# A new written order and a new list of VectorE-masked tiles in an attention and FFN kernel on one core

## The chip, the core and the metric

The kernel runs on one core of one Trainium2 chip. A core has five engines with a queue each, which work in the order of their queues: TensorE (PE; its weight loads are shown as PEld), VectorE (DVE), ScalarE (ACT), GpSimd (POOL) and SyncE (SP), which here only issues DMAs. The metric is the time of one execution on the device in microseconds (us); lower is better. Several runs are given by their median.

## The reference, cut to what matters

```
scores = (q @ k.T) / sqrt(64)                    # 8 batches, 8 heads, 576 rows, head size 64
thresh = max(scores, axis=-1) - tau              # tau = 0.02
scores = where(scores >= thresh, scores, -1e9)
attn   = softmax(scores)                         # over the keys
x      = (attn @ v), heads side by side          # 4608 tokens x 512
h      = max(max(x @ w1, x @ w2), x @ w3)        # 512 -> 768
out    = h @ w_out                               # 768 -> 512, float32
```

Only scores within 0.02 of their row's maximum survive.

## The kernel before, in words

**Tiling.** The structure repeats by batch: a batch has two quads of four heads. A quad's queries are cut into 9 chunks (the last batch is cut in two parts, line 34), and a chunk has two score tiles (r = 0 and 1, one for each pair of heads) of 128 rows by 576 keys. That makes 16 quads, 144 chunks and 288 score tiles. When both quads of a batch are done, its FFN follows: 18 hidden pieces (6 column blocks times w1, w2, w3) and three output pieces.

**The way of a score tile.** TensorE multiplies into one of four PSUM banks (`scores`, line 279). VectorE takes the row maximum (`maximum`, line 311). Then there are two ways. A *masked* tile (line 314: its digit in MASKED is 1) is copied to SBUF as z by VectorE while it takes the maximum; ScalarE takes the exponential of z (line 327); and VectorE multiplies z by (z >= exp(-tau)) and sums the row (`numerators`, lines 333 to 335). In the other way ScalarE reads the bank itself, with a Prelu that flattens all above the threshold (line 329), and takes the exponential and the sum in a second pass (line 337). So a masked tile has two passes on VectorE and one on ScalarE, the other kind one and two. After both tiles of a chunk VectorE takes the reciprocals, POOL multiplies z by them into P (bf16, line 346; six P buffers, four sets of z buffers), and SP turns the chunk's P by a DMA transpose into `ptq` (line 356). A product (`product`, line 358) needs all nine transposed chunks of its quad; VectorE and ScalarE evacuate it to x.

**What sets the order.** ORDER (line 38) is the program written out by hand, letter by letter; `issue` (line 596) emits one piece for each letter, and every engine gets its instructions in that order (`_Ordered`, line 80). On an engine's queue nothing overtakes. The letters by queue:

- TensorE: S score tile, T transposes of q or k (needed before the quad's first score tiles), O product, F first half and B second half of an FFN piece. The digit after S, T, O and F is the PSUM bank. A bank can be written again when its last reader is done.
- VectorE: m maximum, k mask and sum (masked tiles), r reciprocals, c evacuation of k, v maximum of hidden pieces, w evacuation of a product.
- ScalarE: e exponential or Prelu, n exponential and sum (other tiles), a evacuation of q, h evacuation of the first hidden piece, u of output pieces, x of products.
- POOL: p half of a P, q copies of q with its halves exchanged, y casts of v, z casts of the weights.
- SP: t transpose of a P, l one of eight loads of the next quads, g load of weights, o stores.

The letter n or k after an e must fit the tile's digit in MASKED, so the two lists belong together. An FFN piece of a batch can start only when the batch's four products are evacuated; the first needs 36 score tiles.

Of the kernel before, what the change touches and what calls it, by code (L numbers as in the profile page):

```python
# [21 lines left out]
FLAT = 2.0 ** -100  # L22

MASKED = """
101001010100010100100100100001010100000101000011000101010100000100100100
000000111101010100001000101000001100100011011000110011000010100010010001
000100110011000100111000010000101001001100011110000100100010010000111010
100100101111001001000001000110110001100001010111001110011100100001101100
"""


# [4 lines left out]
PBUFS = 6  # L36

ORDER = """
lllS0lmyS1eyS2lmlS3kelmnS0lmegS1repmgS2kyemnS3pT0meS1tmeymaS3S2knS0llremplekT3pnlrS1meqmnpmteprceT2qketS3pS0
anT1rmS2lpnmS3qlempntrcS2pekT1eptS0mnqmelprkalS3petS1mnS2qrmnS0lperlmpetkpeT3mnlS1pmetS2mpnremptekyS0nS2qmlT  # L40
1nzrcaemT1pS3ekpteS0mnS2yrmqelcplnS3rplnmS1tpemS2epmS0tepmS1nrS3mptekpT0erlekO2qtamnpS0melpmleS1kteT3rmnpS0l
nqmleprwnS1qeS2pmtnS0mpeO1czntrmnpS3wekT0permT2aptkeS0pxS3rcnS1gpmtnS2rpmepmetS0mqnO3qmegprnS2wynS0mS1etprmO
3epkeztxS2mewmpF3egS0kpeS2rnBmzF1tmhnkyS3egS2rpmBeF0pnvpBtemF1nkT3zBevF2akS0pghBmnF3tS1rvepBmnpS2F0rveqtS1mp
BmS3ezremF2pghkS1zetBmnF0vS3epgBnmF2pS1vetBmT0hS3rcpeF1S2rmpBmpteF0vpeBknS3ztF1nmS2vyeT3gzBmlO0hrlpalnpF1wle
T3ytBcnS0kS2nlmzO3nlrmeqlvelS2pS0rwxrmyF1npmS3gqBekqeF2vntpBmnS0pS1hmpgeS2mpeS3rmpeF0tmpeBrnS1pvS2tepmF0nzS3
metBrmpT2nS1vpaS3tnS0zmS2ermtpF1nkpnmS3eByrtmepkepF2lemlukS0utkBermnpoT1rekpoS0ecO3lupmtnpO1weoqurktpnS3T0xr
wS2mapoF1meT3qlS0cetBqmF3phS2kleqBmlF1nyF0lrnvBelpBrvS3yhpS2mnF1ptmS0epBmeF2ptvnF3BkeS1tvBnS0mhF2rmepS3rBepm
S1nytvF0peS3mpBnlmS2yetvT3eF1maS0lkBeqlS3mhlF2rmeplT1nlcpS0eBlrmpF1tnS3kpeBmnlO0qvernvtpT2S3wapS1nrmF2ptnS0m
qBempF3hS1kqteO2meykT0rxrBwpceS2yvnS0ylmF1nlS3pmelF2pmtBeBkpeS0vhlS3nrtmF1pS2mepBrlmeF3ptS0vepS2mnBtmF1evnT2
lS0kuS3lakS1onF2rmpemlepS0rkepBtmnpmF3erqktepT1uBuconqroS0yuS2pumoS1pT3mteS0ympeO2koayntmO3ewqelrkS1qxlT2wS0  # L50
rnmlpF3mlepcS1BleyF0tmphS2kpeBlmF3nF1lyveBtrknBpS0vhS2lpnrmF3S1pmetBpmeS0veS1tF2mnS3meBlmnF1F0lveBrelkpS2lBh
mF3npF1vBetkS0nrrBvpF2mhpS3BeptmS1nyvT0T3nrmO2parcyetpS0ewqS3mnO1pmeptkeS2qT3xwS0mayF1meqF3kBeqBrnvT2pS0hclS
1ynmtF3nS2mpBelmpF1elS0vetBmnF3rS2veplBmnpF1S0rhkptBemF3nprS2vleBpmS0tnpvF1emS3tuS2rkepS1nrF0mopnmepS3tmeS2p
rmBeptmeykS1yelS2mupS3lumO1temekT0oeF2ronwplakT3nT1qcS0nBpmnqtraS3peO1mqukuqonT0wS3rocpxS2lmeF0ptrF1mepBkpS3
thBremS0plvF2eptS3mS1ymeBlmF0pelS3veBmF2thS1keBknF0lmF3nlBveBlrknF2plS1rhvBnpmF3nS0pvtBepmF2rS1vtepBmpF0hT3k
tBerS2pavS1npF3mS0qmteBrmepO2vnpeS1twnS3mS0nF2meS1meBrmF0phS3knpBemO2eqvterkpT1xT0wS3caF2pnmT1qBtnrcF0pnvS3q
lBempF1lhS2rkyleBtmF0pvS3epBlrnmS1ypnvF2pterS3mpuS0meS2ptF1meymetS3knS0keBomnrmS2eplS3umpF0luroemptS2ekpT1em
T3oBakteqcT1nS2klaS3rmulpO1umoqeorkyeS0S2npmO3nprtwepmS1xpT0wtnmF2qS3ecpBlermF0qlhkS1pteBmnF2S3pvleBymlnF1vS
0eBtnmF2hS3keBlrmpF1nlvF0pnBlrpS2etvBynmS3S1hlrpmF2erpS0mteBpmeS3pvtnF0S1myeyF2pmeBktBeF3khT1vBaS2vnT0qS1rmp
O3meqcepS2wnF0tS1rnmpT3nmBpS2arvpS1temF3qeO0mpeketT2kxBnwS1clF0hrlmS2pnlBrkyeF3lmF1BrveqlBkpnF0lS2vhlBprmT3t  # L60
S1pvaS2pmeF0tS3mpeBkpteF1vnS2pmulS0moS1eF3metrmepS2knpS1S0nmBertmpekpS1nF2mertmpeS0kepS1mBuuqmtnS0keO3omeoku
O1urkoperowT2xpwT0cS3aqtS1nmF2qrF0myepBekS3yBhmF1pnS2vqteBmpnT0F3rcpelS2vBpnlS0mtphS1meS3mteF2knBmleS0lrnvpS
1ermF2plnS3pmteBpmF1eS0rveptBmnpF2kS3htBemF1nS0rvpleBmpF2nlrS3vpelT0mBtpaS1khS3qtmS0eqO2nmekerS3mpS1nmpO0ewt
ermpF2xwT3kpeF0cnBF1ntvT3BnkBarvS2phT3rrF0mqS1pceBmqtT3nS2pvS1ampS0eF3mpteF2mqeBkByeT1vhS0cT3pS2amF1qtnmF3qe
BkqBevS0nrF2vpT1rmupS3noS2cpnS0mpF1etmyeyrmpS2etkBepmnS3ktuS0urmF2peompnorS1kpeS3tmeS0BpmemteS1kuS0urS3kopnO
2ormepeO1pmnpweO0twrxmO2pxkS1eptS0xmnF3mS2teBkF0hmF1nBkS3ervF2peBmpBveS0ytF3hmS1F2emBkF0eBrvnpBrF1vphS3kpBtF
2mF0pveBytS3nyvO1kO2xrmF1xpBrkepS2BhmF3nptF0vepBF1ntvBS2hBmF3vS0eBrmpF1F2vpeBnS3thS0mBmF1eS3veBmnF0vO2urkepo
O1S0xpS3mF1tmekS0eBmweF3rkpnkuS2pnBorrmupteF0pF1hF2nopvF0tuvpF1rhF2pvF0tvF1phF2vF0tvF1hF2uvF0ovF3hoF1vF2vF0h
F3vF1vO2uoO0wF3xF1F2hF0vF1vF2hF0vF1vF2hF0vF1vF2hF0vF1vF2hF0vF1vF2hF0vBvF1uuooBF2uuouoo
"""  # L70


# [627 lines left out]
```

## Time and profile before

| | before |
|---|---|
| median of 3 runs | 466.03 us (464.69 to 467.4) |
| profiled execution, span from first to last instruction | 465.6 us |
| TensorE busy | 437.9 us (94%) |
| VectorE busy | 403.9 us (87%) |
| ScalarE busy | 394.0 us (85%) |
| GpSimd busy | 318.7 us (68%) |
| DMA packets | 87.44 MB, mean 188 GB/s |
| chain that ended last | PE 70%, DVE 11%, ACT 11%, issue 5%, DMA 2% |

The profile is of one execution. Its slices are 40 equal parts of the span, 11.64 us each; a digit is the busy share in tenths, and PEclk is the granted TensorE clock, in tenths of full speed. A group's row gives line, engine, operation, the tile written and those read, the count, then after the bar the busy time, the mean duration in ns, and the idle time just before, with what ended it. All instructions stand at L89, the line of the helper that records them, so they are told apart by tiles: `sc` scores, `z` and `unused` the outputs of the passes over a score tile, `ptq` the transposed P, `ph` and `po` the FFN's banks, `o` the product. Time of a queue's issuing is shown as SPq. The median is of other runs than the profiled one.

### The profile page before, as it was taken

How to read it: one execution, taken by the hardware profiler on the slowest of the kernel's cores; microseconds unless marked ns; L12 is line 12 of the kernel's file. 1: busy time of each engine (PE TensorE's matmuls, PEld its weight loads, DVE VectorE, ACT ScalarE, POOL GpSimd, SP SyncE). 2: the span in 40 equal slices, each digit the busy share in tenths (PEclk: the TensorE clock that was granted, in tenths of full speed). 3: DMA queues.
4: the chain of work that ended last, by engine and by line, in shares of the span. 5: the costliest groups of instructions: out<-in, count | busy, mean ns of one | idle time of the engine just before them, and what ended most of it. 6: DMA issues, size and time to landing. Idle time of an engine off the chain costs nothing.

```text
span 465.6 us, 14101 instructions
## 1 busy us (share of the span) xinstructions
PE 437.9 (94%) x5188; PEld 314.1 (67%) x5188; DVE 403.9 (87%) x1115; ACT 394.0 (85%) x794; POOL 318.7 (68%) x416
## 2 busy tenths in 40 slices
PE   7778788999999999979999999999999999999995
PEld 5444545666686777648678676877776777787872
DVE  3987899889999989949999899999999999887641
ACT  3998999789999998849988999988999989866622
POOL 3699788699878878556685687767776597462500
PEclk8995899999999999979999999999999999999999
DMA  8999999799999999996999699999979949654702
GB/s 256 242 210 232 199 222 246 166 237 275 216 232 183 212 161 230 221 215 135 207 214 229 130 189 212 212 196 220 160 190 224 153 84 223 105 102 66 173 32 103
DMA packets 212773, 87.44 MB, mean 188 GB/s; under 512 B 185824, under 2 KB 199648, under 8 KB 212704
## 3 DMA queue, kind: packets, MB, share of 16 engines
q1 hardware_dynamic: 212144, 85.95, 89.6%
q8 instruction: 41, 0.67, 0.6%
q10 hardware_dynamic: 560, 0.59, 0.5%
q14 instruction: 28, 0.23, 0.1%
HBM read 34.60 MB, written 9.44 MB: 95 GB/s over the span
## 4 chain that ended last, share of the span: by engine, by line
PE 70%; DVE 11%; ACT 11%; issue 5%; DMA 2%; POOL 0%; SPq 0%; ACTq 0%; DVEq 0%; POOLq 0%
PE sc L89 25%; PE ph L89 25%; ACT z L89 9%; PE po L89 8%; PE o L89 8%; DVE z L89 6%; PE tp L89 3%; DVE unused L89 2%; DMA ptq<-P 1%; DMA qm<-in_q_dram 1%; DVE kt L89 1%; DVE hT L89 1%; ACT xt L89 1%; ACT hm L89 1%; DVE hm L89 1%
## 5 line engine op out<-in xcount | busy, mean ns | idle before, releaser
L89 POOL TENSOR_SCALAR P<-z,rs 128x576 bf16<-128x576 f32 x288 | 229.5, 810 | 94.7 <-DVE rs L89 58.5
L89 PE MATMUL sc<-kt,qt 64*128 64x320 f32 (+2 forms) x640 | 192.7, 442 | 4.2 <-ACT z L89 2.2
L89 PE MATMUL sc<-kt,qs 64*128 64x256 f32 (+2 forms) x640 | 189.7, 431 | 6.2 <-ACT z L89 4.1
L89 PE MATMUL ph<-xt,w 64*128 64x288 bf16 (+2 forms) x2160 | 170.9, 283 | 1.2 <-DVE xt L89 0.3
L89 PEld LDWEIGHTS <-w 64*128 64x128 bf16 (+1 forms) x2160 | 125.0, 94 | 41.1 <-issue 12.6
L89 ACT ACTIVATE z<-sc,nm 128x576 f32<-128x576 f32 x179 | 129.9, 739 | 21.1 <-DVE unused L89 15.5
L89 DVE TENSOR_SCALAR_CACHE_REDUCE unused<-sc 128x576 bf16<-128x576 f32 x179 | 132.2, 749 | 8.2 <-PE sc L89 7.0
L89 ACT ACTIVATE z<-z 128x576 f32<-128x576 f32 x179 | 121.3, 680 | 0.3
L89 PEld LDWEIGHTS sc<-kt,qs 64*128 64x128 f32 (+1 forms) x640 | 93.2, 182 | 27.3 <-ACT z L89 7.4
L89 PEld LDWEIGHTS sc<-kt,qt 64*128 64x128 f32 (+1 forms) x640 | 93.1, 182 | 18.2 <-ACT z L89 6.7
L89 DVE SCALAR_TENSOR_TENSOR z<-z 128x576 f32<-128x576 f32 x109 | 93.3, 861 | 1.0 <-ACT z L89 0.9
L89 DVE TENSOR_SCALAR_CACHE_REDUCE z<-sc 128x576 f32<-128x576 f32 x109 | 81.1, 750 | 11.7 <-PE sc L89 9.9
L89 ACT ACTIVATE z<-z,nm 128x576 f32<-128x576 f32 x109 | 82.0, 771 | 9.8 <-DVE z L89 9.7
L89 POOL COPY qs<-qt 64x640 f32<-64x640 f32 (+1 forms) x62 | 46.9, 756 | 21.8 <-ACT qt L89 18.6
L89 PE MATMUL po<-wo,hT 64*128 64x512 bf16 (+1 forms) x480 | 54.2, 356 | 0.1
L89 ACT ACTIVATE hm<-ph 128x576 bf16<-128x576 f32 (+2 forms) x54 | 32.1, 595 | 16.2 <-PE ph L89 15.9
L89 DVE TENSOR_TENSOR hm<-ph,hm 128x576 bf16<-128x576 f32 (+2 forms) x54 | 36.9, 684 | 9.9 <-PE ph L89 9.1
L89 PE MATMUL o<-ptq,vb 128*64 128x64 bf16 (+2 forms) x544 | 40.6, 288 | 3.4 <-DMA ptq<-P 3.1
L89 PEld LDWEIGHTS <-hT 64*128 64x128 bf16 (+1 forms) x480 | 30.2, 97 | 17.6 <-issue 3.9
L89 DVE TENSOR_TENSOR hT<-ph,hm 128x576 bf16<-128x576 f32 (+2 forms) x54 | 37.0, 685 | 2.9 <-PE ph L89 1.4
L89 PEld LDWEIGHTS <-vb 128*64 128x64 bf16 x544 | 22.9, 113 | 20.9 <-issue 8.5
L89 ACT ACTIVATION_READ_ACCUMULATOR z<-z 128x1 f32 x179 | 35.4, 198 | 0.0
(32 smaller groups left out, 279.9 us busy)
## 6 DMA issues: line engine op xcount, KB each, us to landing
vm<-in_v_dram SPq DMA_DIRECT2D x32, 256.0 KB, 4.4
out_dram<-ob SPq DMA_DIRECT2D x32, 256.0 KB, 2.7
qm<-in_q_dram SPq DMA_DIRECT2D x15, 512.0 KB, 4.4
km<-in_k_dram SPq DMA_DIRECT2D x15, 512.0 KB, 5.5
stage<-in_moe_w_dram SPq DMA_DIRECT2D x9, 512.0 KB, 4.5
ptq<-P SPq DMA_TRANSPOSE x144, 3.9
stage<-in_moe_w_out_dram SPq DMA_DIRECT2D x3, 512.0 KB, 5.9
qm<-in_q_dram SPq DMA_DIRECT2D x16, 64.0 KB, 2.4
```

Of the source, the lines that this page charges most:

```text
L89: ins = fn(*a, **kw)
```

## The change

MASKED and ORDER are replaced; nothing else is touched. MASKED has 120 ones in place of 109. ORDER has the same number of every letter but k (120, not 109) and n (168, not 179), in a new sequence, with new bank digits. The FFN pieces, products and transposes come in the same sequence among themselves. The list of masked tiles, and of ORDER the opening and the lines around the thirteenth product (the 13th O):

```diff
 MASKED = """
-101001010100010100100100100001010100000101000011000101010100000100100100
-000000111101010100001000101000001100100011011000110011000010100010010001
-000100110011000100111000010000101001001100011110000100100010010000111010
-100100101111001001000001000110110001100001010111001110011100100001101100
+011010000100111001001100100001010100101011100001000011010001000110000110
+000011101100101100100001000010110000011111001110000101000010110100100000
+110111011010100000011000100110001001011001010001100110000000111001001100
+001011011001010001001001000110100000100110001100011110110101111001111001
 """
...
 ORDER = """
-lllS0lmyS1eyS2lmlS3kelmnS0lmegS1repmgS2kyemnS3pT0meS1tmeymaS3S2knS0llremplekT3pnlrS1meqmnpmteprceT2qketS3pS0
-anT1rmS2lpnmS3qlempntrcS2pekT1eptS0mnqmelprkalS3petS1mnS2qrmnS0lperlmpetkpeT3mnlS1pmetS2mpnremptekyS0nS2qmlT
-1nzrcaemT1pS3ekpteS0mnS2yrmqelcplnS3rplnmS1tpemS2epmS0tepmS1nrS3mptekpT0erlekO2qtamnpS0melpmleS1kteT3rmnpS0l
-nqmleprwnS1qeS2pmtnS0mpeO1czntrmnpS3wekT0permT2aptkeS0pxS3rcnS1gpmtnS2rpmepmetS0mqnO3qmegprnS2wynS0mS1etprmO
+lllggllS0lylS1mleS2lmlS3emzlnkS0eT1mS2azmeS1rmqeS0mS3eqknpS2mnprmeptemT1yyekT0ylT2acS3leylcpS0nrlmpngS1kynpm
+S2errmepS3lnmpS0lnT1mpS2temS3pemqamqekS1qS3erkqeT0tmpnS2kpermepkepS1tmnS3rncplnS2mplemtT0emS1errktpeS3kpamnT
+2pS0mnpS1trermepmteqS3kepS0lmnS1pmtnpcS0ermtS2peS3mnpmnS0rkeptemS1pemO3ztemqnkS2gerkpgeS0rwtpnS1mpS3nmtS2pnr
+mepmeS1prmeO0pnkptekT2zeS3mtazkS1xS2rwemqtS0nmpS3emptemqemlynrklnpgkeplO1eltlO2wtrrpT0wxT3lcT1laS2lcnS0qmS3n
+pF1meyS2ymeBplmeplS0rkegS3ptmhS2pnmF1nrBmpeS3vqF2emF0peBrkyeT1BvaS3zkhS2nmF1pgS0nmtqBempF3ertvBpeS2rvpnS1mF0
...
-lS0kuS3lakS1onF2rmpemlepS0rkepBtmnpmF3erqktepT1uBuconqroS0yuS2pumoS1pT3mteS0ympeO2koayntmO3ewqelrkS1qxlT2wS0
-rnmlpF3mlepcS1BleyF0tmphS2kpeBlmF3nF1lyveBtrknBpS0vhS2lpnrmF3S1pmetBpmeS0veS1tF2mnS3meBlmnF1F0lveBrelkpS2lBh
-mF3npF1vBetkS0nrrBvpF2mhpS3BeptmS1nyvT0T3nrmO2parcyetpS0ewqS3mnO1pmeptkeS2qT3xwS0mayF1meqF3kBeqBrnvT2pS0hclS
+plkT1BlaklnrmtS2puS1rumpS0eomF3pntkpemS2eT1trmBpecqelS0kpulT1uS2moqaS3mteS1rmnpO0lmnptkeO3ewerkpS2xS0wqmnF1q
+mT3teF2prcBeBpkhS3npvF0ntS1mF2meBtrBepvS3hpS1mnF0tmnS2BrempF1evpBeS3tvnS0rmS2npS1omepF3mF0eytymBBkhF1lekT3lB
+avF2lnF3lvF0okBT1rhpBceByvS2ynpS1mqtO3meqrrvepF2wnS0pknT1S3ptamBqS1mhS0pmeO2emterkpT3xlS1wrpcelS2mlpnF3lS0mq
...
```

More of the change, by code (lines that the diff above doesn't have):

```diff
@@ L38 @@
 ORDER = """
-lllS0lmyS1eyS2lmlS3kelmnS0lmegS1repmgS2kyemnS3pT0meS1tmeymaS3S2knS0llremplekT3pnlrS1meqmnpmteprceT2qketS3pS0
-anT1rmS2lpnmS3qlempntrcS2pekT1eptS0mnqmelprkalS3petS1mnS2qrmnS0lperlmpetkpeT3mnlS1pmetS2mpnremptekyS0nS2qmlT
-1nzrcaemT1pS3ekpteS0mnS2yrmqelcplnS3rplnmS1tpemS2epmS0tepmS1nrS3mptekpT0erlekO2qtamnpS0melpmleS1kteT3rmnpS0l
-nqmleprwnS1qeS2pmtnS0mpeO1czntrmnpS3wekT0permT2aptkeS0pxS3rcnS1gpmtnS2rpmepmetS0mqnO3qmegprnS2wynS0mS1etprmO
-3epkeztxS2mewmpF3egS0kpeS2rnBmzF1tmhnkyS3egS2rpmBeF0pnvpBtemF1nkT3zBevF2akS0pghBmnF3tS1rvepBmnpS2F0rveqtS1mp
@@ L44 @@
[L44 to L48, printed above, removed]
@@ L49 @@
-qBempF3hS1kqteO2meykT0rxrBwpceS2yvnS0ylmF1nlS3pmelF2pmtBeBkpeS0vhlS3nrtmF1pS2mepBrlmeF3ptS0vepS2mnBtmF1evnT2
-lS0kuS3lakS1onF2rmpemlepS0rkepBtmnpmF3erqktepT1uBuconqroS0yuS2pumoS1pT3mteS0ympeO2koayntmO3ewqelrkS1qxlT2wS0
-rnmlpF3mlepcS1BleyF0tmphS2kpeBlmF3nF1lyveBtrknBpS0vhS2lpnrmF3S1pmetBpmeS0veS1tF2mnS3meBlmnF1F0lveBrelkpS2lBh
-mF3npF1vBetkS0nrrBvpF2mhpS3BeptmS1nyvT0T3nrmO2parcyetpS0ewqS3mnO1pmeptkeS2qT3xwS0mayF1meqF3kBeqBrnvT2pS0hclS
-1ynmtF3nS2mpBelmpF1elS0vetBmnF3rS2veplBmnpF1S0rhkptBemF3nprS2vleBpmS0tnpvF1emS3tuS2rkepS1nrF0mopnmepS3tmeS2p
@@ L54 @@
[L54 to L68, printed above, removed]
@@ L69 @@
-F3vF1vO2uoO0wF3xF1F2hF0vF1vF2hF0vF1vF2hF0vF1vF2hF0vF1vF2hF0vF1vF2hF0vBvF1uuooBF2uuouoo
+lllggllS0lylS1mleS2lmlS3emzlnkS0eT1mS2azmeS1rmqeS0mS3eqknpS2mnprmeptemT1yyekT0ylT2acS3leylcpS0nrlmpngS1kynpm
+S2errmepS3lnmpS0lnT1mpS2temS3pemqamqekS1qS3erkqeT0tmpnS2kpermepkepS1tmnS3rncplnS2mplemtT0emS1errktpeS3kpamnT
+2pS0mnpS1trermepmteqS3kepS0lmnS1pmtnpcS0ermtS2peS3mnpmnS0rkeptemS1pemO3ztemqnkS2gerkpgeS0rwtpnS1mpS3nmtS2pnr
+mepmeS1prmeO0pnkptekT2zeS3mtazkS1xS2rwemqtS0nmpS3emptemqemlynrklnpgkeplO1eltlO2wtrrpT0wxT3lcT1laS2lcnS0qmS3n
@@ new lines @@
+pF1meyS2ymeBplmeplS0rkegS3ptmhS2pnmF1nrBmpeS3vqF2emF0peBrkyeT1BvaS3zkhS2nmF1pgS0nmtqBempF3ertvBpeS2rvpnS1mF0
+pF3tmepBkT1zhBtceS2qvS0nztF1mnF3meBtrBepvS2hpS0mnF1tmF3nBkeF0grnvBpgBevpT2S1rrakptS3hS2mpnS0mlpeO1lrmpetmepO
+3wezknT2zS1wngcF0tnmpS2xrBrpmeS3gvpeS2tmS1qnF0mqeBmzeS3veF2lymyS0nlptBkepS1mhF3znmF2lBerkptBevS0pnS1vtnS3rrm
+F2pnmpeS0mepS1lmepBrkeplmT3tpuS0knF1mulaklS2eS0rlmpeS3lmByetmepkS2uS3trempO0kepknyO2lyrnwpumlpS0xtrwS1epmS3m
+pF2etF0mqeBkqBhF1evT2oBncT3F0aorvT2nBoqcS3tnqkF1hpS2mtS0pmeF3mBelBrvepF2tnS1vpBnrmyS0thS3mepS2mpS1emF3etmF0e
@@ new lines @@
+BknS2lveBlrnrT3vpS1lampF0oF3meqlBkeplT2BthcqS1nrS0vpnS2lmplF3nmlpF1etmByeBrvpS2htkS0pnS3meO1memeS2weF0rkpT1T
+3aBmynqO1vtnqrkepS0cnS2ptwmxF3pmeBtrS1repvS0mpF2lS3myetBmeF1ykpF0hS3ekpBnmBtnS2vnF3merrS1vpuS2empoS0mF3eplke
+plkT1BlaklnrmtS2puS1rumpS0eomF3pntkpemS2eT1trmBpecqelS0kpulT1uS2moqaS3mteS1rmnpO0lmnptkeO3ewerkpS2xS0wqmnF1q
+mT3teF2prcBeBpkhS3npvF0ntS1mF2meBtrBepvS3hpS1mnF0tmnS2BrempF1evpBeS3tvnS0rmS2npS1omepF3mF0eytymBBkhF1lekT3lB
+avF2lnF3lvF0okBT1rhpBceByvS2ynpS1mqtO3meqrrvepF2wnS0pknT1S3ptamBqS1mhS0pmeO2emterkpT3xlS1wrpcelS2mlpnF3lS0mq
@@ new lines @@
+etBmpeS1rvnS0plS2mnlpF3melF1ymeBlBretvpS2hkF0pnF3knBmS1eBveS2trrvpS0mpF3mpS1uemF3plemekS0lnT2tmF1arkpntS2kpe
+BmetkeBkuturrS2puS0umpS3nmS1ptemS0pemO2lemlntrO3pweyekoqT1xwS2rqcnoT0S3ymapF1mS0eqtBmpeF2hkpT3BecqF1nvF0nS3r
+ptBnmBpnvS2thS3rrmpeS1mF0peS2myetBmeS3pveS1pkF0nF2mtnBmeF3rBkepBvhpS1nvS2tF0mF3mBelBrevpoF2ohkpT1S0laBmlnF3l
+vnS1lS0nmlBerlmpO2tekpervpS1trF0wpF3mpS2BeqmBnqkS1hS2pmleO0meorveptF1wxkT3nT2cBtaF0vnqT3S2cnqBmnS1pS3hmtF2em
+F0eBrkpeT3S1vpaBknyS2trvpF3rmyS0uymS3eF1mpepemtS2npS0meS3qtmBermepF0knypknT2tukBerrrpculS3upT1umS2ptaS0meqS1
@@ new lines @@
+mepS3mS0eptmT2npO1cnlerO2mlpelkqetwS3qxS0wpnmS1lmS2elF3tmeF0mBelBkhF1nrvpF3nBkpBevS0thrS2pmnF1mlpF3eBketF0vn
+BBnvS2hrrS1rpmS3ymF0epmBeptS2vepS1nmS3ptF0nmpS2emBlyemF1oF3evBektS0hkT2BaklT1nO2lrvpnlmpnO3lcetwT1xwT0rrnS2l
+pclS3amqoF0mS1poeBompeS2tvpeS3rmS0yopS1metF2pmeF3qmBeBqkhF0qekF2nBrvpBnkF1ythyT3vBaS2pvnF0mtnS3S1rmepBrrpeF2
+vnptmS3upS0emS1ptnmF2peketmS0S3nmBelrkpermS1puS0umptS3emS2peF1mqteknS0mnBmerkpeS2kupO3ektnO0rmpnwquT2wrxrpS3
+ceT1pS0tmaF2mqS1elBpmeF3phktS0eBqmT2nplF1vnS0lcBelmF3nlS2rvpleBlrmS1phtS0mnyS3pmeF1tpemF2BekBevF0nktBnvS3nS1
@@ new lines @@
+rmpS2hmF3yepmS0eBtrrmepF1vpT2eBlkapS3lvnS0plF2rnmlpS1mlBepS3mlhyS0lmeS2lrqemtS3eqkO1epmnO0pmlewytyeT2wkF1xT3
+nrcBpnF0vyF2akBnqS1vqBrrtS3mphF0mpeT2BcepS1vnS2ptmT3S0pamF1eoqmF3eBqkoBevS2ohF0tmnF1nT3T2tcBaBnvqS3tnrrT2rpv
+F0ecqS1umpS2myeS0tpmF3epmepktS1eS2pknS0omnBomnterF1mpurrkpuS2eptS3meBpmeptkeS0pS2nmS3tnmS0emO2errkpeO3pmunyw
+pS0txwrS2pumF3eplmS1eBplkS2lhmS0elmF3teF1kBeBrmntpO2vnpO0kxytS3xeF2mF0rvBepBkhyF1yvpS3F2ktS0mBBmS3rhvpS0emF2
+peS1mtBemF3ekF0oeBvBoS1vO2kO3kxS2xrmhpF3kF0peBnmtBF1nrkpF2nBvpBrhvpF3tF1vpBtF0vF2rBpBhpBevS3tS1vS0moO2moeO3m
@@ L70 @@
+eF1wxkS0ueS2mF3mekeS1kF0mBrrkepnpkBnptupF2uF1htF3vF2rrvpF1hF3pvF2vF1pthF3uvpF2vF1htF3vF2vF1hoF3vF2ovF1hF3voF
+2voO1uoO3uowoF0xF2F1hF3vF2vF1hF3vF2vF1hF3vF2vF1hF3vF2vF1hF3vF2vF1hF3vBvF2uuooBF1uuouoo
 """
```

## Prediction, made before the changed kernel was run

> **What bounds the kernel now.** I read the page's slices first, then the busy time by stage, then the chain of waits with a window around its longest transfer, then the groups by shape. I also laid the letters of ORDER beside the trace: on each engine the n-th instruction of a kind is the n-th letter of that kind, so every letter has a time.
>
> ```profile
> PE   7778788999999999979999999999999999999995
> DVE  3987899889999989949999899999999999887641
> ACT  3998999789999998849988999988999989866622
> PEclk8995899999999999979999999999999999999999
> ```
>
> Three parts show. In slices 1 to 7 (to 80 us) TensorE has holes while ScalarE and VectorE are nearly full: there is no FFN piece yet. From slice 8 on TensorE is full, but for one hole in slice 17. At the end only TensorE has work. By stage (columns: stretch, length, then busy time of PE, PEld, DVE, ACT, POOL, the granted clock, the DMA share, GB/s):
>
> ```profile
> 93.00:195.00 102.00, 101.07 (x1256) 72.87 (x1253) 96.28 (x266) 96.58 (x197) 83.12 (x108) 1.00 1.07 216
> 195.00:215.00 20.00, 16.79 (x196) 11.58 (x192) 12.68 (x34) 12.43 (x24) 10.98 (x17) 0.83 0.91 187
> 215.00:388.00 173.00, 172.28 (x2180) 128.23 (x2176) 165.67 (x456) 160.11 (x324) 125.23 (x166) 1.00 0.94 187
> ```
>
> TensorE leads outside the hole, with VectorE and ScalarE 4 to 7% behind it. TensorE's work is the same letter for letter in both orders (288 S, 60 T, 36 O, 186 F, 142 B). So the change can gain in two places, the opening and the hole, and it can lose wherever TensorE is made to wait.
>
> The hole, in the chain of waits from 180 to 215 us, and by stretch:
>
> ```profile
> 198.15 5.35 DMA ptq<-P
> 203.50 0.04 issue
> 203.55 2.61 PE o L89 x14
> ```
> ```profile
> 200.00:203.60 3.60, 0.43 (x3) 0.05 (x4) 1.52 (x5) 2.71 (x6) 3.44 (x6) 0.86 0.75 155
> 203.60:206.00 2.40, 2.40 (x19) 1.26 (x19) 0.00 (x0) 0.00 (x0) 1.01 (x3) 0.50 0.88 260
> 206.00:208.00 2.00, 2.00 (x10) 1.49 (x8) 1.19 (x2) 0.00 (x0) 0.00 (x0) 0.50 1.11 213
> 208.00:210.00 2.00, 2.00 (x20) 0.94 (x20) 1.77 (x6) 1.41 (x2) 0.00 (x0) 0.65 1.04 199
> ```
>
> The thirteenth product (O) waits for the 63rd transpose of P. TensorE idles 3.1 us, then runs at half clock for 4.4 us and at 0.65 for 2 us. The hole's price is 3.1 + 2.2 + 0.7 = 6.0 us.
>
> Why was the transpose late? Its P was ready at 189.5 us, by the letters, yet it was issued at 198.15. SP's queue, in order of time:
>
> ```profile
> 182.91 1.86 SPq L89 DMA_TRANSPOSE ptq<-P  x1
> 184.86 0.55 SPq L89 DMA_DIRECT2D out_dram<-ob  x1
> 185.50 1.36 SPq L89 DMA_TRANSPOSE ptq<-P  x1
> 186.92 1.52 SPq L89 DMA_DIRECT2D vm<-in_v_dram  x2
> 188.48 1.53 SPq L89 DMA_DIRECT2D vr<-in_v_dram  x2
> ...
> 195.54 5.95 SPq L89 DMA_TRANSPOSE ptq<-P  x2
> ```
>
> SP issues without a pause from 175 to 201 us. A transpose holds it for 1.35 us (median), a load or store for about 0.6. Between the end of a P and the issue of its transpose lie 0 us at the 30th chunk and 9.3 us at the 61st: **a backlog on SP**, which no engine's row shows. Once issued, a transpose lands in 3.2 to 7.7 us.
>
> **The masked tiles.** 11 tiles change their way:
>
> ```profile
> L89 ACT ACTIVATE z<-sc,nm 128x576 f32<-128x576 f32 x179 | 129.9, 739 | 21.1 <-DVE unused L89 15.5
> L89 ACT ACTIVATE z<-z 128x576 f32<-128x576 f32 x179 | 121.3, 680 | 0.3
> L89 DVE SCALAR_TENSOR_TENSOR z<-z 128x576 f32<-128x576 f32 x109 | 93.3, 861 | 1.0 <-ACT z L89 0.9
> L89 ACT ACTIVATE z<-z,nm 128x576 f32<-128x576 f32 x109 | 82.0, 771 | 9.8 <-DVE z L89 9.7
> ```
>
> The first pass on VectorE costs the same either way (749 or 750 ns), so VectorE gains 11 x 0.861 = 9.5 us (403.9 to 413.4 busy). ScalarE loses 11 x (0.739 + 0.680 - 0.771) = 7.1 us (394.0 to 386.9). Both stay under TensorE's 437.9, so by totals nothing reaches the path. By place: the ones in MASKED are 21 and 24 after 60 score tiles, 29 and 33 after 84, 63 and 72 after 180, 98 and 104 after 264, 109 and 120 in all (before and after).
>
> The added multiply collides with POOL. In the trace a P pass takes 1.08 us where such a multiply runs beside it for over 0.3 us (56 of them) and 0.74 us where none does (199); the multiply itself takes 0.91 us beside POOL and 0.75 alone. Eleven collisions are 11 x (0.34 + 0.16) = 5.5 us over two queues, and VectorE's part is already in the 861 ns. POOL idles 1 to 6 us in each 20 after 80 us, which hides its part; in the opening POOL is nearly full and has no such cover.
>
> The Trainium skill ("SBUF — State Buffer", section "Who interferes with whom") says that a VectorE operation with two SBUF inputs and a GpSimd operation that reads SBUF exclude each other, the later one blocking fully. By that rule a collision would cost up to a whole pass, some 0.75 us, and eleven 8.2 us instead of 5.5; the trace shows the exclusion, at two thirds of that price on average, and the sum keeps to the trace.
>
> **The opening.** I add up each queue's letters to the eleventh F, where TensorE has become the bound in before (92.9 us). The steps are the mean times from start to start on the queue without its idle time: m 0.69, k 0.81, r 0.09, v 0.67, c 0.68 on VectorE; e 0.66 (0.70 masked), n 0.69, a 0.55, h 0.55 on ScalarE. Before: 64 m, 21 k, 29 r and the few rest make VectorE 74.2, and 64 e, 39 n and the rest make ScalarE 77.1. After: 63 m and 23 k give VectorE 75.0; 62 e and 36 n give ScalarE 73.8. The fuller queue falls from 77.1 to 75.0: **-2.1 us**. The bounds: -3.3 if only ScalarE counts, and +3 if POOL and SP hold it up (rival three). I take -2.1, as ScalarE idles only 1.9, 1.2 and 0.7 us in the stretches from 20 to 80 us. TensorE's work left at that point is larger by 0.5 us (one S): **+0.5**.
>
> **The hole.** From the 27th F to the 63rd transpose, a stretch with TensorE work of 51 and 52 us, SP has 19 transposes, 24 loads and 5 stores in before, 21, 16 and 4 in after: 2 x 1.35 - 9 x 0.6 = 2.7 us less. More than that, their order differs. In before the last seven transposes have eight loads and four stores between them; in after one load. A transpose without loads behind it leaves SP over a microsecond per chunk (a chunk takes about 3 us) to catch up. TensorE's work between P and O is 10.5 us in both. Before needed 14.0 (189.5 to 203.5). After, even with all the rest of the backlog carried along, it is 8.6 - 2.7 + 5.3 = 11.2, a wait of 0.7; with the backlog drained, none. Bounds: 0 to -6.0; I take **-5.5**. What is late next there: TensorE itself.
>
> **New waits.** In the other products the time from P's end to the landing was 3.2 to 9.0 us in before. The cover by TensorE's letters is over 8 us in most of after's (in the first and third, where TensorE is not the bound, VectorE and ScalarE have 10 and 7.7 us of work). Thin are the 21st (6.0 us; before needed 7.5 there and had 7.5), the 33rd (4.8; needed 4.5) and the 35th (5.1; needed 4.0). I put them at **+1.0** (bounds 0 and 3).
>
> The Trainium skill ("TensorE: Matmul & The Clock Gate", "Part 1: The HAM clock gate") ties the half clock to an idle window of some 3.4 us; by it these short waits would cost no clock, and the +1.0 stands. The row speaks for more: from 20 to 60 us the clock is 0.80 and 0.78 though no wait is over 2.3 us, so a wait could cost twice its length, and the term would be +2.
>
> **VectorE beside TensorE.** From the eleventh F to the last S, VectorE has 313.1 us of letters in before and 318.7 in after, TensorE 321.5 and 319.4 (steps: S 0.52, a half of a hidden piece 0.49, of an output piece 1.29, O 1.35, T 0.25 to 0.31). Before kept pace from 225 to 388 us with VectorE's letters at 1.005 of TensorE's; after has 1.007 over nearly the whole way. I take **+0.5** for more small waits; the far bound is all 9.5.
>
> **Sum.** Profiled span 465.6; -2.1 + 0.5 - 5.5 + 1.0 + 0.5 = -5.6, so 460.0. The median of the runs shown lies 0.4 above the span (466.03; 464.69 to 467.4): **460.4 us**.
>
> **The rivals.**
> - VectorE becomes the bound (slower). Place: from the 60th to the 264th score tile, where the extra masks stand and VectorE idles only about 1 us in 20. It decides once VectorE's waits exceed what TensorE's way leaves: 339.5 us from the eleventh F to the last S, less the hole's 6, less 318.7, is 15 us or 4.4%. For it: from 215 to 388 us VectorE idled 7.3 of 173, 4.2%. Against: most of these waits are for S (9.9 and 7.0 us in the groups' rows), and shrink when VectorE is late. If they stay, the 9.5 show in full, the opening's gain is gone and the hole closed: 466.0 + 9.5 - 5.5 = 470.0. Chance 0.2.
> - The hole moves (no change). SP's total is the same, so a backlog may meet another product with a cover of 6 us: -2.1 + 0.5 + 0.5 leaves 464.9. Against: loads are spread with fewer of them just ahead of a product's last transposes. Chance 0.13.
> - The opening gives its gain back. For the 8th to 17th chunk after writes P into a buffer whose transpose was issued only 5.1 to 7.5 us of work earlier (before: never under 9), and lag plus landing took 0.9 + 4.7 there. With 0.5 us for each of ten, +5: 465.4. Chance 0.07.
> - More than forecast: small waits shrink too, as after leaves more work between a bank's release and its reuse (36 under 0.8 us after the eleventh F, against 53): 455. Chance 0.1.
> - That the change doesn't do what it says is out: both orders have 2756 letters, alike but for 11 n that became k.
>
> The forecast itself has 0.5. A measurement of this kernel can tell about 0.5%, 2.3 us. Faster by more takes the forecast, the larger gain and 0.02 of the second and third: 0.62. Within it lie 0.17 of these two; slower are the first and the last 0.01: 0.21. The range of 8 in 10 goes from 453, a little below the larger gain, to 470, the slower rival's price.
>
> **What would show it.** Right: no wait for ptq over 1 us near 200 us, the clock there at 1.00, the first F before 70 us (72.4 before), SP's queue with gaps. Wrong: a TensorE wait for VectorE's z or unused between 100 and 400 us adding up to over 5 us, VectorE at 98% there, or POOL waiting for a transpose in the opening.

## The result, and the profile after

Over 20 runs each the changed kernel takes 469.58 us, the kernel before 466.42; the ratio is 1.0064 (95% interval 1.0044 to 1.0084). It is **slower by 0.64%, 3.0 us**, where 460.4 was forecast. One run of the changed kernel took 1605 us and is left out of the ratio. The profiled execution has a span of 467.6 us and took 469.4: in these runs a time lies 1.8 us above its span, so the profiled execution of before (span 465.6) took 467.4.

The slices of the profile after that answer to those of before:

```profile
PE   7657879998999999999999999999999999999995
DVE  3998999998999999999889999999999998997641
ACT  3979979898999889988998899989999899674522
PEclk9998999999999999999999999999999999999999
```

The hole of slice 17 is gone, from TensorE's busy time and from its clock. By stage (columns as in the prediction: stretch, length, busy PE, PEld, DVE, ACT, POOL, the clock, DMA share, GB/s), the opening of before, then the opening of after and the stretches around the former hole:

```profile
20.00:40.00 20.00, 13.56 (x105) 8.34 (x104) 17.71 (x54) 18.11 (x39) 19.08 (x25) 0.80 0.99 207
40.00:60.00 20.00, 16.86 (x130) 10.51 (x128) 16.34 (x49) 18.84 (x39) 16.09 (x22) 0.78 1.07 235
60.00:80.00 20.00, 17.96 (x214) 11.29 (x210) 19.13 (x53) 19.29 (x41) 18.96 (x23) 1.00 1.14 227
```

```profile
20.00:40.00 20.00, 13.87 (x112) 7.97 (x111) 19.36 (x55) 17.37 (x36) 17.87 (x22) 0.91 1.14 221
40.00:60.00 20.00, 15.31 (x126) 7.52 (x126) 18.78 (x59) 19.59 (x41) 18.93 (x23) 1.00 1.01 203
60.00:80.00 20.00, 16.60 (x200) 10.95 (x200) 19.45 (x52) 17.04 (x35) 18.37 (x23) 1.00 0.91 222
...
160.00:180.00 20.00, 18.85 (x209) 12.22 (x207) 20.00 (x53) 17.21 (x33) 15.61 (x19) 1.00 0.86 186
180.00:200.00 20.00, 19.91 (x284) 15.78 (x281) 19.09 (x51) 17.95 (x38) 11.99 (x16) 1.00 1.11 217
200.00:220.00 20.00, 19.94 (x250) 14.35 (x248) 19.30 (x56) 17.56 (x35) 17.32 (x23) 1.00 0.76 175
```

Around 200 us TensorE works through at full clock. But VectorE is busy for all 20.00 us from 160 to 180, while TensorE is not; and in the opening VectorE is busy for 57.59 of 60 us (the sum of the three stretches) where in before it was for 53.18. The groups of the masked way, first POOL's passes in before, then POOL's and VectorE's in after (after the bar: busy us, mean ns, idle before; VectorE's of before stands in the prediction):

```profile
L89 POOL TENSOR_SCALAR P<-z,rs 128x576 bf16<-128x576 f32 x288 | 229.5, 810 | 94.7 <-DVE rs L89 58.5
```

```profile
L89 POOL TENSOR_SCALAR P<-z,rs 128x576 bf16<-128x576 f32 x288 | 238.2, 841 | 89.4 <-DVE rs L89 52.4
L89 DVE SCALAR_TENSOR_TENSOR z<-z 128x576 f32<-128x576 f32 x120 | 108.1, 913 | 0.2
```

**Here the forecast breaks.** Not only are there 11 more masked multiplies (k): each takes 913 ns instead of 861, and each pass over P on POOL 841 instead of 810, although the instructions are the same. VectorE's busy time rises by 12.5 us, to 416.4, and POOL's by 11.0.

To see where time is lost I take TensorE's **lag** at the n-th F (the first half of an FFN piece): the time when it starts, less TensorE's letters up to it, at fixed steps near those that the prediction gives. The steps are the same for every kernel, so only differences within a column are to be read. The loss in a stretch is the growth of the lag:

| profile | to 11th F | to 51st | to 71st (the hole) | to 151st |
|---|---|---|---|---|
| before | 38.0 | 5.0 | 7.8 | 5.2 |
| after | 37.9 | 6.9 | 3.3 | 9.9 |

In these two profiles the opening gained nothing (0.1 us), up to the 51st F the new order loses 1.9 us more, at the hole it gains 4.5, and after it it loses 4.7 more, in waits so small that the view of waits hardly names them. Together that is the 2.0 us by which the span grew.

### The profile page after: what moved, and what is told of

It reads as the page before. It is cut to its first block, busy times and chain, and to the rows that moved or that the text cites. A ratio compares the mean times of both kernels' runs of the same rounds, so it can differ in the third digit from the quotient of the medians.

```text
span 467.6 us, 14080 instructions
## 1 busy us (share of the span) xinstructions
PE 435.4 (93%) x5188; PEld 310.8 (66%) x5188; DVE 416.4 (89%) x1137; ACT 388.4 (83%) x772; POOL 329.7 (71%) x416
## 5 line engine op out<-in xcount | busy, mean ns | idle before, releaser
L89 POOL TENSOR_SCALAR P<-z,rs 128x576 bf16<-128x576 f32 x288 | 238.2, 841 | 89.4 <-DVE rs L89 52.4
L89 PE MATMUL sc<-kt,qt 64*128 64x320 f32 (+2 forms) x640 | 186.0, 434 | 7.7 <-ACT z L89 3.0
L89 PE MATMUL sc<-kt,qs 64*128 64x256 f32 (+2 forms) x640 | 182.9, 423 | 7.7 <-ACT z L89 3.7
L89 PE MATMUL ph<-xt,w 64*128 64x288 bf16 (+2 forms) x2160 | 165.9, 283 | 1.5 <-ACT z L89 0.4
L89 ACT ACTIVATE z<-sc,nm 128x576 f32<-128x576 f32 x168 | 120.9, 739 | 21.6 <-DVE unused L89 10.2
L89 DVE TENSOR_SCALAR_CACHE_REDUCE unused<-sc 128x576 bf16<-128x576 f32 x168 | 122.2, 749 | 6.7 <-PE sc L89 6.5
L89 ACT ACTIVATE z<-z 128x576 f32<-128x576 f32 x168 | 112.9, 677 | 0.0
L89 DVE SCALAR_TENSOR_TENSOR z<-z 128x576 f32<-128x576 f32 x120 | 108.1, 913 | 0.2
L89 ACT ACTIVATE z<-z,nm 128x576 f32<-128x576 f32 x120 | 90.3, 770 | 11.4 <-DVE z L89 10.6
L89 DVE TENSOR_SCALAR_CACHE_REDUCE z<-sc 128x576 f32<-128x576 f32 x120 | 88.6, 751 | 10.1 <-POOL P L89 8.7
L89 PEld LDWEIGHTS <-hT 64*128 64x128 bf16 (+1 forms) x480 | 30.3, 97 | 19.6 <-issue 6.6
L89 ACT ACTIVATION_READ_ACCUMULATOR z<-z 128x1 f32 x168 | 32.8, 195 | 0.0
```

Of the source, the lines that this page charges most:

```text
L89: ins = fn(*a, **kw)
```

## The experiments

My theory from here on: where k runs beside a pass of POOL, the two together take longer (a *collision*; most are with a pass over P), the new order lets them meet more often and where nothing hides it, and this turns a gain into a loss. A k that runs beside POOL for over 0.3 us took 914 ns (73 of 109) in before and 963 ns (91 of 120) in after, and 750 or 751 where they do not meet; a P beside a k took 1084 (56) and 1130 ns (71), and 744 or 746 alone. I call the time over these lengths the *stretching*. The rivals: the number of masks by itself (VectorE's total), and the z buffers. Each ratio is to the kernel before, run on the same chip.

| label | what | median us (before beside it) | ratio [95%] |
|---|---|---|---|
| e1_after_109 | after, 109 masked | 471.34 (466.51) | 1.0094 [1.0060, 1.0127] |
| e2_before_120 | before, 120 masked | 476.97 (466.51) | 1.0195 [1.0145, 1.0245] |
| e3_before_loads | before, four loads moved | 463.23 (466.51) | 0.9935 [0.9905, 0.9966] |
| e4_after_onein | after, k with one input | 455.64 (466.51) | 0.9753 [0.9717, 0.9788] |
| e5_before_onein | before, k with one input | 462.99 (467.86) | 0.9898 [0.9842, 0.9954] |
| e6_after_z5 | after, a fifth set of z | 472.74 (467.86) | 1.0111 [1.0055, 1.0167] |
| e7_before_loads_120 | e3 with 120 masked | 471.01 (467.86) | 1.0069 [1.0032, 1.0107] |
| e8_loads_onein | e3, k with one input | 460.01 (467.91) | 0.9843 [0.9806, 0.9879] |
| e9_after_onein_early | after, the first 22 k with one input | 464.81 (467.91) | 0.9950 [0.9927, 0.9974] |
| e10_after_onein_late | after, the other 98 with one input | 460.45 (467.91) | 0.9852 [0.9814, 0.9890] |

Differences between two kernels of the table, or between one and after, are taken between their ratios, times 466.4 us. Worked out from the two intervals, the 95% interval of such a difference is some 1.4 to 3 us either way; it is given where it matters.

### e1 and e2: the number of masks alone

In after, 11 masked tiles are turned back (digit 1 to 0, k to n in its place); in before, 11 others are masked (0 to 1, n to k). One tile of each:

```diff
 after -> e1
-pF1meyS2ymeBplmeplS0rkegS3ptmhS2pnmF1nrBmpeS3vqF2emF0pe
+pF1meyS2ymeBplmeplS0rnegS3ptmhS2pnmF1nrBmpeS3vqF2emF0pe
 before -> e2
-3epkeztxS2mewmpF3egS0kpeS2rnBmzF1tmhnkyS3egS2rpmBeF0pnvpBtemF1nkT3
+3epkeztxS2mewmpF3egS0kpeS2rnBmzF1tmhkkyS3egS2rpmBeF0pnvpBtemF1nkT3
```

> The changed order with 11 of its 120 masked tiles turned back (their k letters made n in place; every other letter stands). Theory VectorE: the added masks made VectorE the bound after the opening. VectorE's busy time falls from 416 to about 406 us and the time from 469.6 to 464 to 466, at or under the kernel before. Theory order: the new sequence costs, because POOL's passes stand nearer to the next use of z (8.7 us of VectorE waits for P). The time stays within 1.5 us of 469.6, and those waits stay at 7 us or more.

> The order before with 11 more masked tiles (11 n letters made k in place, spread over the run). Theory VectorE: VectorE's busy time rises by about 10 us to 414, and the time by 3 to 7 us, to 469 to 473. Theory order: VectorE idles about 1 us in 20 there and ScalarE is relieved, so the time moves by less than 1.5 us from 466.4.

e1 is a miss for the theory VectorE: with VectorE relieved of 8.5 us of busy time (407.9) it is no faster than after, its ratio 0.3% above. Taking masks out in place does not bring back what after lost. Each remaining k still took 912 ns, and 81 of 109 met POOL. e2 is slower by 1.95%, 9.1 us, more than either theory had expected and nearly all of the 11 x 0.861 = 9.5 us that VectorE has more to do; in its profile, which is of a run of 479.5 us, the wait for `ptq` is 5.2 us. In both directions a tile turned in place costs time: letters and masks belong together, so neither run isolates the masks' price.

### e3: the hole alone

Four load letters (the 65th to 68th l) are moved from before the 63rd transpose to behind the 13th product, in the old order:

```diff
-...kpeBlmF3nF1lyveBtrknBpS0vhS2lpnrmF3... ...O2parcyetpS0ewqS3mnO1pmeptkeS2qT3xwS0mayF1...
+...kpeBmF3nF1yveBtrknBpS0vhS2pnrmF3...  ...O2parcyetpS0lewqS3lmnO1pmeptkeS2lqT3xwS0lmayF1...
```

> The order before with four load letters moved from ahead of the 63rd transpose to behind the thirteenth product; nothing else is touched. If the hole has the price that the prediction gave it, the wait for ptq near 200 us goes, the clock there is 1.00, and the time falls by 5 to 6 us to 460 to 461.5. Rival: VectorE and ScalarE are behind by then and the hole's time was partly theirs; the wait goes, but the time falls by 1 to 3 us only.

The slices of its profile:

```profile
PE   7776788999999999999999999999999999999995
PEclk8999999999999999999999999999999999999999
```

The hole is closed, and `ptq` is waited for once, for 0.5 us. It brings 0.65%, **3.0 us** [1.6, 4.4], not 5 to 6. Its lag shows why: from the 51st to the 71st F it loses 5.0 us where before lost 7.8, so 5.0 of before's 7.8 are lost there without a hole too. A reading that fits, but was not tested apart: while TensorE stood still, the other engines caught up, and what it would have waited for afterwards was ready. SP's backlog as the cause of the hole is shown; its price was half of the forecast. Of the kernels that compute all, this one is the fastest: it beats both before and after.

### e4 and e5: no collisions

In both orders k becomes an operation with one SBUF input. It writes only the mask and its sum; the masked exponentials are left out. Everything else is issued as it was.

```diff
-            vector.scalar_tensor_tensor(out=zn, in0=zn, scalar=thr, in1=zn,
-                                        op0=OP.is_ge, op1=OP.mult, accum_out=acc)
+            vector.tensor_scalar(out=zn, in0=zn, scalar1=thr, scalar2=None,
+                                 op0=OP.is_ge, op1=OP.add, accum_out=acc)
```

> The changed kernel with the masked tiles' second VectorE pass reading z once instead of twice (it writes the mask and its sum, not the masked exponentials: that part of the computation is left out, and the attention weights are then wrong). Theory collisions: the pass takes about 750 ns instead of 913, P about 750 instead of 841, VectorE's busy time falls by 15 to 20 us, and the time by 5 us or more, under 465. Theory order: the durations fall, but the time stays within 2 us of 469.6, as the waits are for letters and not for VectorE's work.

> The kernel before with the masked tiles' second VectorE pass reading z once (mask and sum only; the masked exponentials are left out, so the weights are wrong). By the profiles VectorE's passes and POOL's P last 31 us longer than alone in before, 47 us in after, and without that after gained 14 us. Theory collisions: before gains in proportion, some 9 us, to 457 to 458; then after without collisions (455.6) is the faster one, and the collisions by themselves turn the change's sign. Theory order: before gains as much as after or more (453 or less), and after stays slower by 3 us without collisions too.

The groups of e4, to set beside those of after above:

```profile
L89 POOL TENSOR_SCALAR P<-z,rs 128x576 bf16<-128x576 f32 x288 | 210.3, 744 | 110.7 <-DVE rs L89 66.1
L89 DVE TENSOR_SCALAR_CACHE_REDUCE z<-z 128x576 f32<-128x576 f32 x120 | 87.7, 744 | 0.2
```

89 of its 120 k run beside POOL for over 0.3 us (91 in after), but no stretching is left: 744 ns for both. In e5 the two take 744 and 747 ns. Alone, the two-input k takes 750, so the form itself saves only 120 x 6 ns = 0.7 us. The new order becomes 3.1% faster, **14.5 us** (1.9 either way); the old one only 1.0%, **4.8 us** (2.6 either way), where the theory had expected some 9. That is a miss in size, and it is the point: without collisions the new order (455.6) beats the old (463.0) by 1.5%, with them it loses by 0.6%. That all of the new order's loss is in its letters, the rival of e5, falls.

The Trainium skill ("SBUF — State Buffer", section "Who interferes with whom") lets only the port pair that VectorE shares with GpSimd cause contention, as a lock and not as a shared rate. The traces agree: with one SBUF input the stretching is gone altogether, and with two it falls on one of the partners. In after there are 17 places where one k and one P run beside each other for over 0.3 us and meet nothing else. In each of them one of the two keeps its own length (729 to 760 ns), and the other ends 0.53 to 0.62 us behind it. The price of a meeting is not bounded by one pass: the longest k of after, 2.28 us where 0.75 is its length alone, began while a cast of v ran on POOL and ended 0.61 us behind the two passes over P that followed the cast. On average a k beside POOL took 0.21 us more, a P beside a k 0.38.

POOL's copies of q and its casts are stretched in the same way (a copy of q took 778 ns on average in after and 669 in e4). That is some 11 us in before and 13 in after, which the sums of stretching below leave out: the one-input k takes away 41.0 us of POOL's busy time in after (329.7 to 288.7), of which P has 27.9.

### e6: more z buffers

```diff
-ZBUFS = 4
+ZBUFS = 5
-PBUFS = 6
+PBUFS = 5
```

To make room, `unused` and `obr` get one buffer instead of two.

> The changed kernel with five sets of z buffers in place of four; to make room, unused has one buffer, P five and obr one. Theory order (POOL's passes stand too near to the next use of z): the waits of VectorE and ScalarE for POOL's P (about 8.7 and 6 us) go, and the time falls by 3 us or more, to 466.5 or less. Theory collisions: the time stays within 1.5 us of 469.6, as the multiplies still meet POOL's passes.

It is slower than after by 0.5%, 2.2 us, with intervals that overlap, so neither theory's time came out. The waits of VectorE and ScalarE for POOL's P, 8.7 and 6.3 us in after, fell to 0.3 and 1.4, and nothing was won by it; ScalarE's waits for `unused`, which now has one buffer, rose from 10.2 to 15.4. The smaller counts of the three others may thus cost something; this was not tried apart.

### e7: 11 more masks without the hole

e3's order with e2's 11 tiles masked in place.

> The order before with the four loads moved (463.2 us) and with the same 11 more masked tiles as in the second experiment, which cost 10.5 us there. If about half of that was a deeper hole at the thirteenth product, the 11 masks cost 4 to 6 us here: 467 to 469. If VectorE alone is the price, they cost 9 to 11 us: 472 to 474.

Against e3 the 11 masks cost 1.34%, 6.2 us (2.3 either way); against before (e2) they cost 9.1. Some 3 us of e2 may thus have been a deeper hole, but that difference is within the noise; the 6.2 lie just above the first expectation. About two thirds of their 9.5 us of VectorE time reached the end, although VectorE's total stays 20 us below TensorE's.

### e8: neither hole nor collisions, old order

> The old order with the four moved loads (no hole) and the masked multiply with one SBUF input (mask and sum, the masked exponentials left out). It shows what the new order is worth once neither the hole nor the collisions count. If the collisions cost the old order some 5 us wherever the hole is, this takes 463.2 - 4.8 = 458 to 459, and what the new order has over it (455.6) is 3 us. If the hole hid the collisions of the old order (the other engines caught up during it), taking both away brings more than the two alone: 455 or less, and the new order has nothing over the old but the closed hole.

460.01 us, which is 459.1 set against 466.4 for before: the first branch, at its upper end. It lies 0.55% below e5 (2.6 us, 3.1 either way; the hole alone gave 3.0), and the collisions cost the old order 4.3 us without the hole and 4.8 with it. Within the noise the hole's price and the collisions' are independent. The new order without collisions is still 0.9% faster, 4.2 us (2.4 either way). By the profiles it is made in the opening: the 11th F starts at 91.8 us in e8 and at 86.0 in e4, and after it the losses are alike (table below).

### e9 and e10: where the collisions cost

The first 22 masked tiles, or the 98 others, get the one-input k (their masked exponentials are left out):

```diff
+            if 2 * number[g, idx] + r < 55:       # e10: >= 55
+                vector.tensor_scalar(out=zn, in0=zn, scalar1=thr, scalar2=None,
+                                     op0=OP.is_ge, op1=OP.add, accum_out=acc)
+            else:
+                vector.scalar_tensor_tensor(out=zn, in0=zn, scalar=thr, in1=zn,
+                                            op0=OP.is_ge, op1=OP.mult, accum_out=acc)
```

> The new order, with one SBUF input in the masked multiplies of the first 22 masked tiles alone (those up to some 80 us; mask and sum there, the masked exponentials left out), two inputs in the other 98. It places the 14 us that all 120 gave. If the opening bears the price (no engine has slack there, POOL is nearly full, and its multiplies are the longest, 1053 ns), 22 of 120 bring 5 us or more: 464 or less, first F before 69 us. If the price is even over the tiles, 22 bring 2.6 us: 467. If the later places bear it, where VectorE keeps just level with TensorE, it is 468.5 to 469.5.

> The counterpart: one SBUF input in the last 98 masked tiles, two in the first 22. If the opening bears the price, 460 or more; if it is even over the tiles, 469.6 - 11.4 = 458; if the later places bear nearly all, 456 to 457. Where the gains of this kernel and its counterpart add to the 14 us of both, the two prices are independent; where they add to less, an early delay is taken over by a later one.

Against after the first 22 bring 1.14%, 5.3 us, and the 98 bring 2.12%, 9.9 us; together 15.2, where all 120 gave 14.5. Within the noise the prices add up, and a delay in the opening is not absorbed later. The first F comes at 68.3 us in e9, as expected if the opening bears its price. A masked multiply of the opening cost 0.24 us of the whole, a later one 0.10. The opening bears more than its share but not all. The groups in the first 92 us, of before:

```profile
L89 DVE SCALAR_TENSOR_TENSOR z<-z 128x576 f32<-128x576 f32 x21 | 19.3, 919 | 0.9 <-ACT z L89 0.9
L89 POOL TENSOR_SCALAR P<-z,rs 128x576 bf16<-128x576 f32 x56 | 45.2, 819 | 12.7 <-DVE rs L89 8.4 <-issue 3.2
```

and of after:

```profile
L89 DVE SCALAR_TENSOR_TENSOR z<-z 128x576 f32<-128x576 f32 x23 | 24.1, 1059 | 0.1
L89 POOL TENSOR_SCALAR P<-z,rs 128x576 bf16<-128x576 f32 x56 | 45.9, 836 | 3.8 <-DVE rs L89 2.2 <-ACT z L89 0.5
```

Two multiplies more, and 4.8 us more of VectorE; POOL's idle time before P has shrunk from 12.7 to 3.8 us, so the next k nearly always meets it: 22 of 23 did, against 17 of 21 in before. The losses by stretch, for the kernels that tell the parts apart:

| profile | to 11th F | to 51st | to 71st | to 151st |
|---|---|---|---|---|
| e3 (old, no hole) | 35.0 | 5.1 | 5.0 | 5.3 |
| e5 (old, hole, no collisions) | 35.7 | 3.8 | 5.3 | 3.8 |
| e8 (old, no hole, no collisions) | 37.0 | 3.8 | 3.3 | 4.0 |
| e9 (new, no collisions in the opening) | 32.8 | 6.9 | 3.3 | 9.7 |
| e10 (new, none after the opening) | 37.5 | 3.9 | 2.2 | 4.6 |
| e4 (new, none) | 31.7 | 3.6 | 2.3 | 4.6 |

Read by columns: the opening of the new order is worth 3 to 5 us (35.7 and 37.0 in e5 and e8, 32.8 and 31.7 in e9 and e4) only while its multiplies do not collide. It is one profile each, and those of e4 and e5 are of runs 2.1 and 2.9 us under their kernel's median; the old opening with collisions varies from 35.0 (e3) to 38.0 (before). But the new one with them stood at 37.5 and 37.9, without them at 31.7 and 32.8. From the 71st F on, the new order's multiplies cost 5.3 us (9.9 against 4.6), the old order's 1.4 (5.2 against 3.8).

## Why the prediction was wrong

The time, 469.6 us, lies inside the stated range at its slow end, but the change was to be a gain of 5.6 us. The steps from before to after: collisions of the old order out -4.8 us (e5), hole out -2.6 (e8), the new letters with their 11 more masks -4.2 (e4), collisions of the new order in +14.5 (after). They must add up to the measured +3.0, for they are a chain of ratios; the noise of each single step is 1.9 to 3.1 us either way. What counts is which of them the prediction had. In its own terms, by the lags of the two profiles: the opening was to give -1.6 and gave -0.1, the hole -5.5 and -4.5, and all the small waits +1.5 and +6.6.

- **"VectorE beside TensorE", +0.5, is the step that failed**, with the paragraph ahead of it that put 11 collisions at 5.5 us over two queues and took POOL's part as hidden after 80 us. It counted only the collisions of the eleven added multiplies, at the old order's mean, when all 120 stand in new places. The stretching (over 750 and 744 ns) is 12.1 us on VectorE and 19.0 on POOL in before, 19.6 and 27.9 in after: 16.4 us more, not 5.5. And the collisions were not hidden: of these 47.5 us 14.5 reached the end, against 4.8 of 31.1 in before. The difference, 9.7 us, is what was put at +0.5 behind the opening and at nothing in it: of the 14.5 us some 5 fall in the opening (e9) and some 10 behind it (e10). Of the prediction's own bounds the far one, 9.5, is near that in size, but by luck: it was meant as the added work of 11 masks, and taking 11 masks out again won nothing (e1).
- **The hole, -5.5**: mechanism right (e3: only loads moved, the hole gone; after: no wait for `ptq` near 200 us, clock 1.00). The size was off: 3.0 in e3, 2.6 between e5 and e8. The price was taken as wait plus slow clock; that TensorE's later waits become shorter because the other engines work on meanwhile fits the lag in e3, but was not tested apart.
- **The opening, -2.1 and +0.5**: without collisions the new order gives more than forecast, 4.2 us over the whole kernel, and all of it is taken back by the collisions there (e9: 5.3). The first F came at 71.7 us, not before 70. The prediction itself said that POOL has no cover in the opening, yet its letter sums used one step for k, 0.81 us, and nothing for POOL; in after a k takes 1.06 us there, 0.2 more than the mean of before. An estimate from these numbers: 23 k at 0.2 us more bring VectorE's sum from 75.0 to 79.6 us, over the 77.1 of before, so the term would have been a loss. The rival of the opening named P's buffers instead; that POOL would hold it up was right, through which mechanism was not: POOL has no named wait for a transpose there.
- **New waits, +1.0**: they did not come. TensorE's whole idle time for `ptq` at products is 0.8 us in after.
- **VectorE as the bound, the slower rival, 470.0**: nearest in time (469.6) and in place, as the 9.9 us that e10 wins lie behind the opening. But its mechanism was VectorE's added work, and the 9.9 us are collisions. Its point of decision, VectorE's waits used up, was near: VectorE idled 4.6 of 120 us from 80 to 200 (7.8 in before). Its sign, over 5 us of named waits for z and `unused`, did not show: TensorE's waits for VectorE's z from 92 to 420 us sum to 2.4. VectorE was busy for 95% of the stretch from 100 to 400 us, not 98%. Most of the 9.9 us that TensorE loses between the 71st and the 151st F has no name in that view.
- **From span to median, +0.4**: a run's time is 1.8 us above its span, so the profiled execution took 467.4, 1.0 above the median of before. That is small beside the rest.

Some things stay open. The one-input form frees VectorE and POOL at once; which of the two queues carries the price was not tried, nor was the price of the 11 masks by themselves in the new order. Why the multiplies meet POOL for longer in the new order outside the opening (928 ns against 900 beside POOL, 69 of 97 against 56 of 88) is described here and not explained. And e1's small loss against after (0.3%, intervals overlapping) is not explained either.

## What to carry to other kernels

When an order written by hand changes, do not price an interaction between two engines by its mean in the old order: count who meets whom in the new places, and where nobody has slack to hide it. A hole in the bounding engine can be worth less than its width: here moving four loads closed one that was priced at 6.0 us, and won 3.0. To learn what an interaction costs, replace one partner by an operation of the same length that does not interact, in both kernels: that showed a gain under a loss.

## What the runs showed of the hardware

- A VectorE multiply with two SBUF inputs and a POOL pass over SBUF, 128x576 f32 each, took 750 and 744 ns apart; in after the multiply took 963 ns on average beside POOL and the pass 1130 beside a multiply, with single ones of 2277 and 1842. Where only one of each met for over 0.3 us (17 places), one kept its length and the other ended 0.53 to 0.62 us behind it. With one input on VectorE both took 744 ns on average, and none over 754 (e4).
- The same stretching, 31.1 and 47.5 us in sum for k and P, cost 4.8 and 14.5 us of the time: 15% in one order, 31% in the other.
- In before the granted clock fell to 0.50 also where TensorE was partly busy: it was busy for 1.62 us of the 3.41 us that end at 21.66 us, 1.83 of the 3.40 that end at 35.30 and 1.92 of the 3.40 that end at 55.80, with the clock at 1.00 in each, and each is followed by a stretch of 3.4 us or more at 0.50.
